# A delta-rule recurrence and a channel mixer on one core: loads reordered at the start, a join's last products rearranged, later due dates for weight slices

## The chip, the core and the metric

The kernel runs on one core of a Trainium2 chip. The metric is the device time of one execution in microseconds. A time given for a kernel is the median over its runs; a profile shows one execution, whose own time is given beside its span. The engines are TensorE (PE, and PEld for its weight loads), VectorE (DVE), ScalarE (ACT), GpSimd (POOL) and SyncE (SP). POOL, SP and ACT also issue the DMA transfers.

## The reference

Two stages follow each other. The first is a delta rule over 768 tokens, for 4 batches of 8 heads with head size 48; the second is a mixer over tokens (low rank) and channels. All numbers are float32.

```python
k_n = k / (norm(k) + 1e-6)
for t in range(S):
    y[:, :, t] = q[:, :, t] @ state
    v_old = state^T @ k_n[:, :, t]
    state += beta[t] * outer(k_n[:, :, t], v[:, :, t] - v_old)
x = y.transpose(0, 2, 1, 3).reshape(4, 768, 384)
u = x + (x^T @ U @ V)^T              # U 768x32, V 32x768
out = u + relu(u @ w_ch1) @ w_ch2    # 384 -> 1536 -> 384
```

The weights, U and V reach the kernel as float64.

## The kernel before, in words

**Units and chunks.** A batch is cut into two units of 384 tokens (`n = 2 b + half`), a unit into six chunks of 64 tokens. Inside a chunk the delta rule is a triangular system: for all eight heads the kernel needs the inverse of a 64x64 unit triangular matrix, kept transposed in `zt`. A unit has 48 such matrices, and they are built like this:

- `load` (L458) brings k, q and v of a unit; `load_beta` (L261) brings beta. For units 0 and 1 q comes as it is and TensorE turns it (`grams`, L519, `turn`, L533); from unit 2 on POOL loads k and q in pieces (`turn_all`, L479, line L495) and VectorE turns them (L504).
- `grams` also makes the products k k^T (`pg`) and k q^T (`qk`), at L562.
- `blocks` (L612) writes `pg` to a scratch in DRAM and reads it back in another layout (`scr<-pg` L634, `gs<-scr` L645), takes the norms (L653 and on), and inverts the diagonal blocks on VectorE in a chain of pairs of operations (L705, L711). For units 0 to 2 the blocks are 16 wide, later 32. The result goes through the scratch again into `zt` (L720, L783).
- `join` (L809) puts blocks together, for units 0 to 2 in three thirds of 16 matrices. Two products with 16-wide blocks (`p_e` L844, `p_d` L856) make 32-wide ones, L860 subtracts, L861 turns the third into `zn` on VectorE, and two products with 32-wide blocks make the off-diagonal block: `p_x` (L867), copied in two halves of 32 partitions on ScalarE (L877), then `p_v` (L883), negated into `zt` in two halves (L889). All of these products are 32x32 tiles of the array. `p_x` and `p_v` have 16 products each, in two of the array's quarters; as float32 products they leave 32 records.

**Recurrence.** `recur(b)` (L906) runs over twelve chunks. Each chunk is a chain across engines: `p_y` from the state (L910), `rhs` on VectorE (L937), `p_s` (L944), `z` on ScalarE (L953), `p_s` (L958) and `p_y` (L966), the new state on VectorE (L981) and the output on ScalarE (L988). A chunk needs its third of the joins.

**Mixer.** `front(b, i)` (L995) makes u for half a batch: `p_tt` (L1008), copied by VectorE (L1014), `p_tt` again (L1017), `p_h` (L1032), added to x (L1038), turned (`p_u`, L1042). `wide(b, i)` (L1053) does the two large products, `p_f` (L1083, with a relu at L1060) and `p_o` (L1104, added at L1065 and stored at L1066).

**Weights.** 14 slices of float64 come in order: four of w1, U, V, two more of w1, six of w2 (`W2` = 8 is the number of the first w2 slice). `start` (L316) issues a load at L337; `one_slice` (L352) turns float64 into float32 with five VectorE operations (L364, L376, L381, L386, L391) and one ScalarE operation (L371). Slices use two buffers, `wide` and `stage` (in two cases an unused part of `w2_sb`), so a load waits until the slice before the last has been converted.

**What sets the order.** A planner written into the kernel. Every part is a generator which yields either a list of events it needs (`need`) or a `step` with its expected cost on each engine. `run` (L158) picks the step that can start first by its own clock; a low place number in `order` (L1116 on) wins when steps compete. `emitted(key, after)` says when an event will be true. So costs and dates in the code issue no work; they decide the order in which instructions stand on each engine. Each engine then works in that order. `fetched` (L146) models that TensorE's instructions come in lots of 256, `ins` being the number in a step. Two gates, `gate` (L413), are small POOL copies that wait for a value of unit 0's inversion (`opened 0`) and for one of the transferred `zt` (`opened 1`); what stands behind them on POOL starts no sooner.

**POOL at the start**, in the order of the program: constants, beta of unit 0, q of unit 0 (8 loads), beta of unit 1, constants and pads (`later_constants`, L244: `quarters`, `mask_e`, `bias_e`, pads of q), weight slice 0, q of unit 1 (8 loads), gate 0, v of unit 0 (8), slice 1, a first four key loads of unit 2 (L495), gate 1, v of unit 1 (8), the remaining twelve.

Of the kernel before, what the change touches and what calls it, by code (L numbers as in the profile page):

```python
# [27 lines left out]
def kernel(  # L28
# [78 lines left out]
    clock = dict(now=0.0, at=0.0, pe=0.0, dve=2.5, act=0.8, sp=0.8, pool=3.8, slow=1.6)  # L107

    LOT, FETCH = 256, 4.1
    lot = dict(since=0.0, used=0)  # L110

# [6 lines left out]
    def step(pe=0, dve=0, act=0, sp=0, pool=0, then=0.0, on=None, take=(), give=(), ins=64):  # L118

        return dict(
            pe=pe, dve=dve, act=act, sp=sp, pool=pool, then=then, on=on, take=take, give=give, ins=ins
        )
# [33 lines left out]
    def run():  # L158

        while waits:  # L160
# [35 lines left out]
            if s["pe"]:  # L196
                fetched(at, s, True)
                ends["pe"] = clock["pe"] = at + s["pe"] * clock["slow"]
            for e in ENGINES[1:]:
                if s[e]:  # L200
                    ends[e] = clock[e] = max(clock[e], ends["pe"]) + s[e]
# [104 lines left out]
    def load_weights():  # L306
# [9 lines left out]
        def start(i):  # L316
            dst, src, groups = slices[i]
            n = dst.shape[1]
            if i in (W2 + 1, W2 + 3):

                at = WIDE * (2 + (i - W2 + 1) // 2)
                wide = early[:, at : at + 2 * n].bitcast(I32)
                wide = wide.rearrange("p (n two) -> p n two", two=2)
            elif i % 2 and i < W2:
                wide = stage[:, 0 : 2 * n].bitcast(I32).rearrange("p (n two) -> p n two", two=2)
            else:
                wide = conv.tile([128, n, 2], I32, name="wide")
            src = src.bitcast(I32)
            to = wide.rearrange("p n two -> p (n two)")
            if groups:  # L330
                to = to.rearrange("p (c r) -> p c r", c=groups)
                src = src.rearrange("(c p) r -> p c r", c=groups)
            copies = 128 // src.shape[0]
            yield step(pool=0.55 * copies)
            for c in range(copies):
                at = slice(c * 128 // copies, (c + 1) * 128 // copies)
                nc.gpsimd.dma_start(out=to[at], in_=src)  # L337
            loaded[i] = wide
            emitted(("sent", i))
            emitted(("landed", i), 6.0)  # L340

        def load_all():
            for i in range(len(slices)):
                last = i - 2 if i < W2 + 5 else i - 1
                yield need(("weights", last), ("q", 0))
                if i > 0:
                    yield need(("opened", int(i > 1)))
                if i == W2 + 1:
                    yield need(*early_used)
                yield from start(i)  # L350
# [107 lines left out]
    def load(n):  # L458
# [12 lines left out]
        if n == 1:  # L471
            yield from load_keys(1)
            yield need(("beta", 1))
# [5 lines left out]
    def turn_all(n):  # L479
# [5 lines left out]
        yield need(("queries turned", n - 1))  # L485
# [33 lines left out]
    def grams(n, place):  # L519
# [24 lines left out]
        def products(c0, i):  # L544
# [4 lines left out]
            yield step(pe=0.6 if n > 2 else 1.1 if n == 2 or i else 0.8, then=0.1, take=banks)  # L549
# [259 lines left out]
    def join(n, third, pg, zt):  # L809

        SB, TQ = BK // 2, CS // 3
# [45 lines left out]
        yield step(dve=1.2, then=-0.75, give=(bank,))  # L859
        nc.vector.tensor_tensor(out=odd, in0=odd, in1=p_d, op=ALU.subtract)  # L860
        turned(zn, zq)  # L861
        yield step(pe=0.65 if n < 2 else 0.55, then=0.4 if n > 1 else 0.1, take=(bank,))
        p_x = ps_of([128, TQ, BK], "p_x")
        for e, (c, j, r) in enumerate(where):
            for g in range(2):
                rows = slice(L * g + BK, L * g + L)
                nc.tensor.matmul(  # L867
                    p_x[L * g : L * g + BK, e],
                    pg[rows, c, j, r, 0:BK],
                    zq[rows, e, BK:L],  # L870
                    start=True,
                    stop=True,
                )
        xz = room([128, TQ, BK], "xz")
        yield step(act=0.75, then=0.1, give=(bank,))
        for g in range(2):
            nc.scalar.copy(xz[L * g : L * g + BK], p_x[L * g : L * g + BK])  # L877
        yield step(pe=0.65 if n < 2 else 0.55, then=0.4 if n > 1 else 0.1, take=(bank,))
        p_v = ps_of([128, TQ, BK], "p_v")
        for e in range(TQ):  # L880
            for g in range(2):
                rows = slice(L * g, L * g + BK)
                nc.tensor.matmul(  # L883
                    p_v[rows, e], zn[rows, e, 0:BK], xz[rows, e], start=True, stop=True
                )
        yield step(act=0.75, give=(bank,))
        for g in range(2):
            rows = slice(L * g, L * g + BK)
            nc.scalar.mul(zq[rows, :, BK:L], p_v[rows], -1.0)  # L889
# [105 lines left out]
    def front(b, i):  # L995
# [7 lines left out]
        if i == 0:  # L1003
# [11 lines left out]
            yield step(pe=0.65, then=0.1, take=("one",), ins=4)  # L1015
# [11 lines left out]
        yield step(pe=0.75, then=0.1, take=("pair", "one"), ins=12)  # L1027
# [8 lines left out]
        def block(e, c):  # L1036
            yield step(dve=0.57, then=0.1, give=((), ("pair",), ("one",))[e])
            nc.vector.tensor_tensor(out=x[:, c], in0=x[:, c], in1=p_hs[e], op=ALU.add)  # L1038
            yield step(pe=0.35, then=0.1, take=("one",), ins=6)
# [76 lines left out]
    order = [(load(0), 2), (later_constants(), 2.04), (recur(0), 2)]  # L1116
    order += [(load_beta(n), (2.02, 2.035)[n] if n < 2 else 2.1 + 0.9 * n) for n in range(2 * B)]
    order += [(grams(0, (2.1, 2.35)), 2.1), (grams(1, (1.97, 2.4)), 1.97)]
    order += [(blocks(0), 2), (blocks(1), 2.52), (load(1), 2.04)]
# [49 lines left out]
```

## Time and profile before

| | |
|---|---|
| median of 8 runs | 655.12 us (650.66 to 660.74) |
| profiled execution: its time / its span | 656.99 us / 655.3 us |
| mean granted TensorE clock | 0.911 of full |
| DMA, mean over the span | 73 GB/s, 47.87 MB |
| p_f (L1083), 576 records | 205.9 us busy |
| p_o (L1104), 576 records | 209.8 us busy |
| first p_s of the recurrence (L944) starts | 49.28 us |
| last rhs of batch 0 (L937) starts | 118.12 us |
| first p_tt (L1008) / first p_f (L1083) starts | 121.37 us / 132.3 us |

The profile's page gives each engine's busy time, then the span in 40 slices of about 16.4 us with a digit per slice for the busy share in tenths. PEclk is the granted clock of TensorE in the same way. The chain of waits follows the work that ended last back from the end; a line has start, length and what it was. A timeline line has start, length, engine, source line, operation, output and input with their shapes, a count, and in brackets how long the engine was idle before and what released it. The table by stages gives, for a stretch of time, each engine's busy time with the number of instructions in brackets (in the order PE, PEld, DVE, ACT, POOL), then the granted clock, the DMA share and GB/s.

### The profile page before, as it was taken

What the parts mean: (1) busy time and instruction counts of PE and PEld (TensorE: products, weight loads), DVE (VectorE), ACT (ScalarE), POOL (GpSimd) and SP (SyncE); (2) the same over time, 40 slices, a digit from 0 to 9 for tenths busy, and PEclk for the clock granted to TensorE, in tenths of its full rate; (3) what the DMA queues carried; (4) which work ended last, traced back from release to release, by engine and by line L of the source; (5) the groups of instructions that cost most, each with busy time, mean ns of one, the idle gap of its engine ahead of it and who ended that gap; (6) DMA issues with size and microseconds to landing.
All of it is one profiled execution on the core that took longest, in us unless ns stands there. A gap on an engine that the chain in (4) does not pass through costs nothing.

```text
span 655.3 us, 20993 instructions
## 1 busy us (share of the span) xinstructions
PE 607.9 (93%) x9312; PEld 381.2 (58%) x9312; DVE 316.8 (48%) x761; ACT 169.2 (26%) x421; POOL 228.4 (35%) x380
## 2 busy tenths in 40 slices
PE   4559878699999999989999999999999999999997
PEld 3458767356655556455655555655565555555554
DVE  3489767885578388427831684388101012000000
ACT  3414444224312321233212321222112211210210
POOL 9654276676452734390557055400000000000000
PEclk9655555789999999979998999999999999999999
DMA  8865455856321812550255026400300000000000
GB/s 129 190 156 126 113 157 112 224 126 121 88 69 38 173 30 56 111 124 3 37 124 122 14 38 119 91 14 2 62 27 14 1 13 13 12 1 24 12 14 24
DMA packets 85163, 47.87 MB, mean 73 GB/s; under 512 B 73584, under 2 KB 78240, under 8 KB 85072
## 3 DMA queue, kind: packets, MB, share of 16 engines
q0 software_dynamic: 14528, 26.98, 17.7%
q1 hardware_dynamic: 65808, 18.86, 13.3%
q8 instruction: 73, 1.20, 0.8%
q10 hardware_dynamic: 4736, 0.69, 0.6%
q14 instruction: 18, 0.15, 0.1%
HBM read 35.49 MB, written 11.01 MB: 71 GB/s over the span
## 4 chain that ended last, share of the span: by engine, by line
PE 84%; DVE 6%; DMA 5%; issue 2%; ACT 1%; SPq 0%; POOL 0%; ACTq 0%; DVEq 0%; POOLq 0%
PE p_f L1083 31%; PE p_o L1104 31%; PE p_y L910 4%; PE p_g L562 3%; PE p_s L944 3%; PE p_s L958 2%; PE p_y L966 2%; PE p_u L1042 1%; PE p_h L1032 1%; PE p_d L856 1%; DVE xt L711 1%; DVE prod L705 1%; DMA wide<-in_moe_w_ch_dram 1%; DMA gs<-scr 1%; PE p_tt L1008 1%
## 5 line engine op out<-in xcount | busy, mean ns | idle before, releaser
L1104 PE MATMUL p_o<-w_sb,h_f 128*128 128x384 f32 x576 | 209.8, 503 | 0.0
L1083 PE MATMUL p_f<-ut,w_sb 128*128 128x384 f32 x576 | 205.9, 504 | 0.0
L1083 PEld LDWEIGHTS p_f<-ut,w_sb 128*128 128x128 f32 x576 | 106.0, 192 | 66.6 <-issue 4.0
L1104 PEld LDWEIGHTS p_o<-w_sb,h_f 128*128 128x128 f32 x576 | 103.3, 191 | 61.4 <-issue 4.0
L1060 ACT ACTIVATE h_f<-p_f 128x384 f32<-128x384 f32 x96 | 47.2, 491 | 181.7 <-PE p_f L1083 181.5
L495 POOL DMA_DIRECT2D qn<-in_k_dram x96 | 58.5, 617 | 56.4 <-DVE prod L705 38.7
L1065 DVE TENSOR_TENSOR x<-x,p_o 128x384 f32<-128x384 f32 x24 | 13.3, 554 | 130.6 <-PE p_o L1104 130.4
L711 DVE TENSOR_TENSOR xt<-xt,prod 96x112 f32<-96x112 f32 (+21 forms) x200 | 63.7, 319 | 6.9
L705 DVE TENSOR_TENSOR prod<-gs,xt 96x112 f32<-96x112 f32 (+21 forms) x200 | 63.0, 315 | 5.1
L434 POOL DMA_DIRECT2D vn<-in_v_dram x64 | 42.3, 671 | 64.2 <-DVE rhs L937 50.8
L495 POOL DMA_DIRECT2D qn<-in_q_dram x96 | 58.8, 623 | 13.0 <-DVE kt L504 9.2
L988 ACT COPY x<-p_y 64x192 f32<-64x192 f32 x96 | 30.1, 313 | 44.3 <-PE p_y L966 42.3
L981 DVE TENSOR_TENSOR s<-s,p_s 128x192 f32<-128x192 f32 x40 | 14.1, 351 | 54.6 <-PE p_s L958 49.8
L937 DVE TENSOR_TENSOR rhs<-vn,p_y 128x192 f32<-128x192 f32 x44 | 15.4, 350 | 47.0 <-PE p_y L910 46.5
L953 ACT COPY z<-p_s 128x192 f32<-128x192 f32 x48 | 15.3, 319 | 78.2 <-PE p_s L944 77.9
L944 PEld LDWEIGHTS p_s<-rhs,zt 64*64 64x64 f32 x704 | 17.1, 152 | 26.2 <-issue 22.8
L434 POOL DMA_DIRECT2D kn<-in_k_dram x48 | 31.4, 664 | 1.1 <-issue 1.0
L944 PE MATMUL p_s<-rhs,zt 64*64 64x48 f32 x704 | 23.0, 248 | 6.9 <-DVE rhs L937 6.3
L958 PEld LDWEIGHTS p_s<-z,kn 64*64 64x64 f32 x704 | 16.5, 153 | 20.7 <-issue 12.0
L910 PEld LDWEIGHTS p_y<-s,kt 48*64 48x64 f32 x704 | 16.7, 152 | 19.3 <-issue 7.5
L966 PE MATMUL p_y<-z,qk 64*64 64x48 f32 x768 | 23.3, 240 | 1.7 <-issue 1.2
L958 PE MATMUL p_s<-z,kn 64*64 64x48 f32 x704 | 22.4, 248 | 2.2 <-ACT z L953 2.2
(126 smaller groups left out, 589.9 us busy)
## 6 DMA issues: line engine op xcount, KB each, us to landing
wide<-in_moe_w_ch_dram POOLq DMA_DIRECT2D x7, 768.0 KB, 6.0
vn<-in_v_dram POOLq DMA_DIRECT2D x64, 72.0 KB, 3.5
out_dram<-x SPq DMA_DIRECT2D x24, 192.0 KB
kn<-in_k_dram POOLq DMA_DIRECT2D x48, 72.0 KB, 3.2
gs<-scr SPq DMA_DIRECT2D x8, 384.0 KB
scr<-xt SPq DMA_DIRECT2D x8, 384.0 KB
scr<-pg SPq DMA_DIRECT2D x30, 96.0 KB
zt<-scr SPq DMA_DIRECT2D x30, 96.0 KB
```

The lines of the kernel that those rows point to most:

```text
L434: engines[queue].dma_start(out=t[half(g ^ (s % 2) if crossed else g), :, s], in_=src[b, 4 * g + s, hf * UC * L : (hf + 1) * UC * L, :].rea ...
L495: nc.gpsimd.dma_start(out=places[rows, x, j, :, 0 : ds.stop - ds.start], in_=src[b, h, hf * UC * L : (hf + 1) * UC * L, ds].rearrange("(m ...
L705: nc.vector.tensor_tensor(out=prod, in0=gb[:, :, j : j + 1, j + 1 :].to_broadcast([NP, split, m, w]), in1=xb[:, :, 0:m, j : j + 1].to_broa ...
L711: nc.vector.tensor_tensor(out=xb[:, :, 0:m, j + 1 :], in0=xb[:, :, 0:m, j + 1 :], in1=prod, op=ALU.subtract,)
L910: nc.tensor.matmul(p[half(x ^ par), par, D * (2 * i + j) : D * (2 * i + j) + D], kq[i][half(par, D), x, j, cu], s_old[half(par, D), x, j], ...
L944: nc.tensor.matmul(p_s[half(x), par, D * (2 + j) : D * (2 + j) + D], zt[half(x ^ par), cu, j, par], rhs[half(x ^ par), 2 * j + par], start ...
L958: nc.tensor.matmul(p_s[half(par), x, D * j : D * j + D], kn[half(x), cu, 2 * j + par], z[half(x), 2 * j + par], start=True, stop=True,)
L966: nc.tensor.matmul(p_y[half(x ^ par), par, D * (2 + j) : D * (2 + j) + D], qk[half(x), cu, par, j], z[half(x), 2 * j + par], start=(c == 0 ...
L988: nc.scalar.copy(tokens_of(b, c, g), pair_of(p_y, 1)[half(g)])
L1060: nc.scalar.activation(hs[f], p_f, ACTF.Relu)
L1083: nc.tensor.matmul(p_f, w1_sb[:, t, f * 128 : (f + 1) * 128], ut[:, t], start=(t == 0), stop=(t == KT - 1),)
L1104: nc.tensor.matmul(p_os[c], hs[e][:, c * 128 : c * 128 + 128], w2_sb[:, e], start=(e == 0), stop=(e == FT - 1),)
```

## The change

- **Loads.** q of unit 1 no longer waits for beta of unit 1, and `load(1)`, `load_beta` and `later_constants` have other places. The first weight slice waits for gate 0, all others for gate 1. `turn_all` of unit 2 waits for gate 1. In the program POOL now issues: beta of unit 0, q of unit 0, q of unit 1, constants and pads, beta of unit 1, gate 0, v of unit 0, slice 0, gate 1, v of unit 1, slice 1, all sixteen key loads of unit 2.
- **Joins of units 0 to 2.** Only the left half of `zn` is turned after the subtraction. `p_x` keeps 16 products: for the first eight matrices into the upper 32 partitions of each half, for the other eight, from `zn`, into the lower ones, so that one copy of 128 partitions with half the elements takes both. `p_v` keeps 16 products too, for the first eight matrices as before and for the others in the other association (`xz` as the weights), alternating between two banks; four negations of half the size follow. In the very first join two of them go to VectorE.
- **Planner.** w2 slices are expected 8.0 instead of 6.0 after their issue; a switch between large and small products costs 0.05 or 0.1 at full clock; a few steps have other costs or other `ins`.

On the engines, the program has as many TensorE instructions as before. On VectorE the first two operations on weight slice 0 stood ahead of unit 0's inversion and now stand in the recurrence with the other three; the first two operations on the second w2 slice stood ahead of the last `rhs` of batch 0 and now stand behind it and behind the turn of unit 2's queries. Around the front of batch 1, where TensorE had p_tt, p_g, p_h, p_u and p_x with no p_o between, seven of the large p_o products now stand among them.

```diff
-    clock = dict(now=0.0, at=0.0, pe=0.0, dve=2.5, act=0.8, sp=0.8, pool=3.8, slow=1.6)
+    clock = dict(now=0.0, at=0.0, pe=0.0, dve=2.5, act=0.8, sp=0.8, pool=3.8, slow=1.6,
+                 big=False)
...
+    SWITCH = 0.05, 0.1
...
+            big=ins < 16,
...
+                if s["big"] != clock["big"] and clock["slow"] == 1.0:
+                    ends["pe"] = clock["pe"] = clock["pe"] + SWITCH[s["big"]]
+                clock["big"] = s["big"]
...
-            emitted(("landed", i), 6.0)
+            emitted(("landed", i), 6.0 if i < W2 else 8.0)
...
-                yield need(("weights", last), ("q", 0))
-                if i > 0:
-                    yield need(("opened", int(i > 1)))
+                yield need(("weights", last), ("opened", int(i > 0)))
...
             yield from load_keys(1)
-            yield need(("beta", 1))
...
-        yield need(("queries turned", n - 1))
+        yield need(("queries turned", n - 1), ("opened", 1))
...
-        yield step(dve=1.2, then=-0.75, give=(bank,))
+        yield step(dve=0.9, then=-0.3, give=(bank,))
         nc.vector.tensor_tensor(out=odd, in0=odd, in1=p_d, op=ALU.subtract)
-        turned(zn, zq)
+        nc.vector.transpose(zn[:, :, 0:BK], zq[:, :, 0:BK])
+        TH = TQ // 2
+        halves = [(slice(L * g, L * g + BK), slice(L * g + BK, L * g + L)) for g in range(2)]
...
-        p_x = ps_of([128, TQ, BK], "p_x")
-        for e, (c, j, r) in enumerate(where):
-            for g in range(2):
-                rows = slice(L * g + BK, L * g + L)
+        p_x = ps_of([128, TH, BK], "p_x")
+        for late in range(2):
+            for e, (c, j, r) in enumerate(where[TH * late : TH * late + TH]):
+                for top, low in halves:
+                    if late:
+                        nc.tensor.matmul(
+                            p_x[low, e], pg[top, c, j, r, BK:L], zn[top, TH + e, 0:BK],
+                            start=True, stop=True,
+                        )
+                    else:
+                        nc.tensor.matmul(
+                            p_x[top, e], pg[low, c, j, r, 0:BK], zq[low, e, BK:L],
+                            start=True, stop=True,
+                        )
+        xz = room([128, TH, BK], "xz")
+        yield step(act=0.35, then=0.1, give=(bank,))
+        nc.scalar.copy(xz, p_x)
...
+        p_vs = [p([128, TH, BK], "p_v") for p in (ps_of, ps_one)]
+        for e in range(TH):
+            for top, low in halves:
                 nc.tensor.matmul(
-                    p_x[L * g : L * g + BK, e],
...
+                    p_vs[0][top, e], zn[top, e, 0:BK], xz[top, e], start=True, stop=True
+                )
                 nc.tensor.matmul(
-                    p_v[rows, e], zn[rows, e, 0:BK], xz[rows, e], start=True, stop=True
-                )
-        yield step(act=0.75, give=(bank,))
-        for g in range(2):
-            rows = slice(L * g, L * g + BK)
-            nc.scalar.mul(zq[rows, :, BK:L], p_v[rows], -1.0)
+                    p_vs[1][top, e], xz[low, e], zq[low, TH + e, BK:L], start=True, stop=True
+                )
+        first = (n, third) == (0, 0)
...
+        for i, p_v in enumerate(p_vs):
+            for top, low in halves:
+                to = zq[top, TH * i : TH * i + TH, BK:L]
+                if first and i:
+                    nc.vector.tensor_scalar_mul(to, p_v[top], -1.0)
+                else:
+                    nc.scalar.mul(to, p_v[top], -1.0)
...
-            yield step(pe=0.65, then=0.1, take=("one",), ins=4)
+            yield step(pe=0.65, then=0.1, take=("one",), ins=16)
...
-        yield step(pe=0.75, then=0.1, take=("pair", "one"), ins=12)
+        yield step(pe=0.75, then=0.1, take=("pair", "one"), ins=16)
...
-            yield step(pe=0.35, then=0.1, take=("one",), ins=6)
+            yield step(pe=0.35, then=0.1, take=("one",), ins=16)
...
-    order = [(load(0), 2), (later_constants(), 2.04), (recur(0), 2)]
-    order += [(load_beta(n), (2.02, 2.035)[n] if n < 2 else 2.1 + 0.9 * n) for n in range(2 * B)]
+    order = [(load(0), 2), (later_constants(), 2.03), (recur(0), 2)]
+    order += [(load_beta(n), (2.015, 2.04)[n] if n < 2 else 2.1 + 0.9 * n) for n in range(2 * B)]
...
-    order += [(blocks(0), 2), (blocks(1), 2.52), (load(1), 2.04)]
+    order += [(blocks(0), 2), (blocks(1), 2.52), (load(1), 2.02)]
```

## The prediction, made before the run

> **What bounds the kernel now.** I read the page first: what share each engine is busy, and how that is spread over the 40 slices.
>
> ```profile
> PE 607.9 (93%) x9312; PEld 381.2 (58%) x9312; DVE 316.8 (48%) x761; ACT 169.2 (26%) x421; POOL 228.4 (35%) x380
> ...
> PE   4559878699999999989999999999999999999997
> ...
> PEclk9655555789999999979998999999999999999999
> ...
> q8 instruction: 73, 1.20, 0.8%
> ```
>
> TensorE is nearly full from slice 9 on (about 132 us), and what it does from there is mostly the mixer's products, which the change leaves alone. Before that, slices 2 to 7, it is partly busy and at half clock. So a gain has to come from the first 132 us, or from holes in the dense stage. The chain of waits up to 50 us shows what sets the start of the recurrence.
>
> ```profile
> 14.34 3.51 DMA scr<-pg
> 17.98 6.09 DMA gs<-scr
> ...
> 25.19 0.20 DVE cp L660
> 25.41 0.25 ACT xt L678
> 25.66 0.81 ACT power L371
> ...
> 26.55 0.20 DVE prod L705
> ...
> 35.13 3.81 DMA scr<-xt
> ...
> 39.32 3.23 DMA zt<-scr
> ```
>
> It is a serial run: two transfers, unit 0's inversion on VectorE (26.55 to 35.1), two transfers, then the first join, which the timeline shows from its last third on.
>
> ```profile
> 45.85 1.06 PE L867 MATMUL p_x<-zt,pg 32*32 32x32 f32 x32 [0.54 <-DVE zt L860]
> 46.96 0.75 ACT L877 COPY xz<-p_x 32x256 f32<-32x256 f32 x2 [2.79 <-PE p_x L867]
> 47.38 1.45 PE L883 MATMUL p_v<-xz,zn 32*32 32x32 f32 x32 [0.46 <-ACT xz L877]
> 48.86 0.77 ACT L889 ACTIVATE zt<-p_v 32x256 f32<-32x256 f32 x2 [1.15 <-PE p_v L883]
> ```
>
> The recurrence starts behind it, at 49.28. Twelve chunks follow, the last one's rhs at 118.12. Its end is spoilt by a transfer: in the timeline VectorE stands in L364 until a w2 slice lands, with rhs queued behind it and TensorE waiting for rhs.
>
> ```profile
> 112.21 0.72 POOL L337 DMA_DIRECT2D w_sb<-in_moe_w_ch_dram  x1
> 117.18 0.56 DVE L364 TENSOR_SCALAR power<-w_sb 128x768 uint16<-128x768 uint16 x1 [3.77 <-DMA w_sb<-in_moe_w_ch_dram]
> 118.12 0.35 DVE L937 TENSOR_TENSOR rhs<-vn,p_y 128x192 f32<-128x192 f32 x1
> 118.61 0.68 PE L944 MATMUL p_s<-rhs,zt 64*64 64x48 f32 x16 [4.05 <-DVE rhs L937]
> ```
>
> The table by stages completes it: 48 to 112 us is at half clock, 270 to 295 us has a hole.
>
> ```profile
> 48.00:112.00 64.00, 53.79 (x1883) 48.03 (x1880) 50.88 (x96) 28.28 (x70) 35.08 (x57) 0.50 0.50 129
> 270.00:295.00 25.00, 22.23 (x417) 12.63 (x418) 7.31 (x13) 8.65 (x21) 21.15 (x33) 0.86 0.67 137
> ```
>
> **The change, part by part** (its own execution: 656.99 us, span 655.3).
>
> **A. Loads at the start.** Unit 1's q is eight issues of 0.66 us on POOL, 72 KB each. They move from 16.1-22.3 to right behind unit 0's q, 10.6-15.9. POOL's 2.8 us of constants and pads (12.8-15.6) and the second beta (2.2 us) slip behind them, to about 18.7 and 21. Who waits: the first transposes of q (17.2) need the pad, so they slip about 1.4 us, with 16 products of k queued behind; their copies sit behind the wait for gs (24.09) on ScalarE anyway, so this is free until gs lands before 20. The second beta is needed at 38.8: free. The first w1 slice (768 KB) leaves the stretch in which gs is read; it goes behind v of unit 0, from 15.6 to about 29. So gs shares the engines with less: it took 6.09 us at 18; the transfer at 416.43, in quiet, let its sqrt start 3.71 us later, the one at 121.72 took 4.25. I take 4.3: -1.8 (bounds -2.4, and +1 if q now slows the scr write before it). The slice's first two operations leave the chain as well: L376 (0.55 us at 25.30) held back L689, on which the inversion waits; prod could start at 26.1: -0.45. Slice 1 and 16 loads of unit 2's keys (9.8 us of POOL) now wait until zt is there, so scr<-xt and zt<-scr are alone with slice 0. The same write at 57.18 and at 458.82 let zt be issued 3.0 us later, against 3.8 here: -0.7. Unit 2's keys then land near 57 and are used at 85.5: free.
>
> **B. The first join.** The p_x copies (two of 0.37) become one over all partitions with half the elements: 0.28 (192 elements take 0.32 at L953, 32 take 0.25 at L678), -0.47. p_v took 1.45 because its second half waited for the second copy; on four quarters I take 0.65, half of p_d's 64 records (1.08, of which 0.24 is the length of a single one): -0.8. The two negations (0.77) are split between ScalarE and VectorE, 0.6: -0.15. p_x keeps its length: each half of it still uses two quarters, and the half that needs the turned zn finds it ready (half a transpose of 0.71, about 0.4, beside the first half). Together -1.4.
> The price of p_v rests on this: p_e puts 64 records on four quarters in about 1.01 us from start to next start, p_x 32 on two quarters in about 1.0, so 16 against 31 ns a record. The Trainium skill (TensorE: Matmul & The Clock Gate, "Wait — 56ns, not 53.3ns?") says that starts never come closer than some 25 ns however small the product. By that rule p_v needs 0.8 us and saves 0.2; by the row of p_e it saves 0.5. The row is the same shape in the same stage: I take it.
> A to B: rhs and all behind it 4.35 us earlier.
>
> **C. Five further joins at half clock.** p_v takes 0.5 less of TensorE each, 2.5 in all. But the instructions stay as many, and TensorE fetches them in 73 blocks over the span (16 KB each, about 255 of its 18,624); its "issue" gaps in 66 to 104 us (1.07, 0.49, 0.85, 1.20, 1.12) stand at such blocks. A faster p_v there only waits longer. I take half: -1.2 (bounds 0 and -2.5). ScalarE: copy 0.28 and four negations of about 0.28 against 1.52: even. VectorE: six half transposes save 1.8, two negations cost 0.5.
>
> **D. Slices and the last chunk.** In the new order the first two operations on the first w2 tile stand behind the last rhs and the turn of q. The wait of 3.77 leaves the recurrence: -3.8. VectorE's load up to that rhs is even: five operations of slice 0 instead of three (+1.1), two of that w2 tile fewer (-1.1). But slice 0 is now converted wholly inside the recurrence, and a load starts only when the last slice but one is out of its buffer; if the recurrence moves up 4 us and the slices by less, the 1.2 us wait at 107.8 grows: +0.5. The last rhs comes 8.9 us earlier, about 109.2. Next late is the w2 tile: issued about 4 us earlier, landing near 113, then four operations (3 us) ahead of the copy of tt, which was at 124.12. That gives back 1.7: tt is 7.2 earlier.
>
> **E. The dense stage.** Three joins at full clock: p_e takes 0.75 for 64 records there, p_v 0.69 for 32, so p_v on four quarters about 0.47: -0.2 each, -0.7 (bounds 0 and -1). The planner's costs of switching, the w2 dates and `ins` issue nothing themselves; they reorder. Around the front of batch 1 the new order puts seven p_o between p_tt, p_h and p_u, where TensorE stood 2.8 us. The clock by five-us stretches (0.92, 0.50, 0.89 from 280 to 295) means 6.9 us at half, 3.4 lost. The skill (same page, "What's actually happening") ties the drop to an idle window of about 3.4 us; the holes here are shorter, each under 1.5 us, and the clock fell all the same. By the rule filling them saves at most 2.8, by the row up to 6.2. I take -2.5, as a second such hole at 345 to 353 (1.3 idle, 1.7 by clock: 3.0) stays to be filled or not; the bound above is +3, another such hole. An order with new delays has waits of its own: +1.5, near the 1.2 row (bounds 0 and +6).
>
> Sum: -7.2 - 0.7 - 2.5 + 1.5 = -8.9. On the profiled execution 648.1; that one lies 1.9 above the median of 655.12, so the median is **646.2**. About 0.5%, 3.3 us, is what a measurement can tell from no change.
>
> **Rivals.**
> 1. *Hidden gain* (0.19): fetches swallow C, q's early loads slow scr as much as gs gains, the hole moves elsewhere. Left are B (-1.4) and part of D (-2): about 652.5. For it: DMA share is 0.9 to 1.2 from 4 to 24 us, so moved bytes only trade places. Against: 768 KB really leave that stretch.
> 2. *Slower, by late slices* (0.11): the two buffers make each load wait for the last conversion but one; slice 2 is issued at 59.4 and its L364 starts at 66.2, one landing (6.0) later, so there is under 1 us to spare. If slice 0's later conversion makes VectorE stand in front of rhs for 2 us at each of slices 2 to 8, that is 7 x 2 = +14: 655.1 - 8.9 + 14 = 660. It decides from about 1.3 us per slice. Against: slice 2's buffer is free at about the same absolute time, as VectorE finishes the inversion earlier. The dense end has room: the last w2 slice is done at 175.0, and the product that needs it comes at about 184.
> 3. *It doesn't do what it says* (part of 1): p_v's two products write the same columns in two banks; if they take turns, B shrinks by 0.5 and C and the -0.7 vanish: 648.6. p_g has that pattern (64 records in 1.09 us at full clock), which speaks against it.
>
> **Chances.** Likeliest case and rival 3: 0.70, faster by over 0.5%; no change 0.19; slower 0.11. From the bounds (A -3.5 to +1, C, E) the likeliest case spans 638.5 to 651.5; stretched over rival 1 the range is 638.5 to 655.
>
> **What would show it.** gs landing within 4.5 us; the first p_s near 45; p_v near 0.65 us; the last rhs near 109 with no L364 wait ahead of it; the first p_f near 125; clock 1.0 through 270-295. Wrong: a first p_s later than 48, L364 waits on slices 1 to 8 summing above 5 us, or a first p_f after 131.

## The result, and the profile after

The changed kernel takes 646.41 us (median of 11 runs, 644.29 to 650.58), the kernel before 653.6 us (median of 32 runs in the same session, 649.79 to 660.74). The ratio is 0.9891, 95% interval 0.986 to 0.9922: 7.1 us less. Disturbed runs are left out of this ratio and of those below. The total is within 0.2 us of the predicted 646.2, but part of that is luck: the prediction started from a median of 655.12 us (8 runs) and took 8.9 off; with 32 runs the median before is 653.6, and 7.1 came off. The parts, too, are not where the prediction put them.

In the page of the changed kernel the second row is TensorE's busy share in 40 slices, the third the granted clock.

```profile
PE 600.8 (93%) x9312; PEld 376.0 (58%) x9312; DVE 315.1 (49%) x763; ACT 167.4 (26%) x428; POOL 229.4 (36%) x380
...
PE   5667687799999999999999999999999999999997
...
PEclk9855555789999999999999999999999999999999
```

From slice 9 to the last but one both rows are nines; before, the busy row had an 8 at slice 17 (counted from 0), the clock row a 7 there and an 8 at slice 21. Slices 2 to 7 look no fuller than before. The table by stages says so in numbers.

```profile
270.00:295.00 25.00, 24.38 (x449) 14.94 (x446) 12.24 (x31) 10.38 (x26) 15.79 (x25) 1.00 0.68 119
46.65:118.88 72.23, 54.70 (x2000) 48.16 (x2001) 55.78 (x105) 30.35 (x83) 41.18 (x66) 0.50 0.56 150
```

The hole at 270 to 295 is closed, with full clock: five p_o products (ten records; the list of the change says seven) now stand between the first p_tt and p_x of that front, as in these lines.

```profile
272.41 0.91 PE L1125 MATMUL p_o<-w_sb,h_f 128*128 128x384 f32 x2
273.25 0.92 PE L1053 MATMUL p_h<-tt,v_sb 32*128 32x384 f32 x6
274.10 0.91 PE L1125 MATMUL p_o<-w_sb,h_f 128*128 128x384 f32 x2
```

The second row of the table is the first recurrence, from the first p_s to the first p_tt: 72.23 us. Before, it ran from 49.28 to 121.37 us, 72.09.

The start, in the chain of waits:

```profile
15.16 4.35 DMA scr<-pg
19.64 3.42 DMA gs<-scr
...
33.81 3.25 DMA scr<-xt
37.44 3.15 DMA zt<-scr
```

gs takes 3.42 instead of 6.09; the scr write ahead of it pays 0.84 of that back and starts 0.8 later. The first join (timeline; p_v has a row per record, of which the first and the last stand here):

```profile
44.11 0.64 PE L883 MATMUL p_x<-zt,pg 32*32 32x32 f32 x16 [0.54 <-DVE zt L866]
...
44.59 0.68 PE L877 MATMUL p_x<-zn,pg 32*32 32x32 f32 x16
...
45.31 0.27 ACT L889 COPY xz<-p_x 128x128 f32<-128x128 f32 x1 [2.87 <-PE p_x L877]
45.62 0.26 PE L894 MATMUL p_v<-xz,zn 32*32 32x32 f32 x1 [0.35 <-ACT xz L889]
...
46.04 0.24 PE L897 MATMUL p_v<-zt,xz 32*32 32x32 f32 x1
...
46.65 0.96 PE L965 MATMUL p_s<-vn,zt 64*64 64x48 f32 x16 [0.37 <-ACT zt L910]
```

p_v runs from 45.62 to 46.28: 0.66 us, where 0.65 was predicted. The first p_s is at 46.65. The end of the recurrence and the first mixer:

```profile
115.52 0.35 DVE L958 TENSOR_TENSOR rhs<-vn,p_y 128x192 f32<-128x192 f32 x1 [1.31 <-PE p_y L931]
...
121.61 0.56 DVE L1035 COPY tt<-p_tt 128x384 f32<-128x384 f32 x1 [0.43 <-PE p_tt L1029]
...
126.80 0.26 ACT L658 ACTIVATE norm<-gs 96x32 f32<-96x32 f32 x1 [7.32 <-DMA gs<-scr]
...
127.61 1.10 PE L1063 MATMUL p_u<-ident,x 128*128 128x128 f32 x6 [1.27 <-ACT ut L1066]
```

The last rhs waits for no slice. But it comes at 115.52, not at 109, and the first p_f follows at 130.85, only 1.4 us earlier than before (132.21). From there to the end before needed 523.1 us and the changed kernel 513.9. The two profiled executions (656.99 and 646.41 us, spans 655.3 and 644.7) are 10.6 us apart, and 9.2 of these lie in the dense stage, for which the prediction had 1.7.

**A ledger of the dense stage.** For every kernel below I took the stretch from the first p_f to the end and split it in three, from the table by stages in steps of 5 us: idle time of TensorE up to its last product, time lost to the clock ((1 - granted clock) x length), and the rest, which is the products at full speed and some 3.7 us after the last one. The clock column has two parts: what was lost in the first 10 us of the stretch, where a half clock from the first mixer's front still runs on, and what was lost later.

| kernel | ratio to before, 95% | first p_s | p_s to p_tt | first p_f | idle | clock | rest |
|---|---|---|---|---|---|---|---|
| before | 1 | 49.28 | 72.1 | 132.2 | 4.4 | 2.7 + 5.1 | 510.9 |
| changed | 0.9891 (0.986-0.9922) | 46.65 | 72.2 | 130.9 | 1.5 | 2.1 + 0 | 510.3 |
| load_only | 0.9984 (0.9959-1.0009) | 47.55 | 71.8 | 129.6 | 5.2 | 0 + 1.7 | 511.1 |
| join_only | 0.9928 (0.9901-0.9954) | 52.22 | 69.9 | 132.9 | 2.2 | 0 + 0 | 509.9 |
| switch_only | 0.9967 (0.9942-0.9992) | 52.40 | 71.9 | 135.0 | 3.4 | 0 + 1.7 | 511.1 |
| w2dates_only | 0.9989 (0.9963-1.0016) | 50.22 | 67.9 | 130.9 | 3.6 | 1.3 + 1.7 | 510.7 |
| load_and_join | 0.992 (0.9887-0.9953) | 46.23 | 73.9 | 130.9 | 2.7 | 2.7 + 3.4 | 509.9 |
| without_w2dates | 0.9919 (0.9885-0.9952) | 45.67 | 73.2 | 129.3 | 2.8 | 0 + 0 | 510.8 |
| without_switch | 1.0001 (0.9965-1.0037) | 46.95 | 72.5 | 131.6 | 6.9 | 2.5 + 5.1 | 510.0 |
| without_join | 0.993 (0.9901-0.996) | 47.89 | 71.2 | 131.4 | 2.2 | 1.5 + 0 | 511.0 |
| old_join_between | 0.9905 (0.9875-0.9934) | 46.93 | 75.1 | 132.6 | 2.0 | 0 + 0 | 510.4 |
| filler_in_hole | 1.0016 (0.9984-1.0049) | 52.26 | 70.4 | 133.4 | 4.3 | 0 + 1.7 | 513.7 |
| pv_three_times | 1.0013 (0.9983-1.0043) | 47.39 | 81.2 | 140.7 | 1.3 | 1.8 + 0 | 510.2 |
| qk_left_out | 0.9873 (0.9835-0.9912) | 47.13 | 68.8 | 128.2 | 2.7 | 2.4 + 0 | 510.5 |

Ratios are from many runs, the other columns from one profiled execution each. A profiled execution can lie off the median of its kernel: those of before, without_switch, switch_only and load_and_join took 2.7 to 4.1 us more, that of without_w2dates 3 less. So a row says where the time of one execution went, and the ratio says what the kernel is worth. The rest lies within 1.2 us in all kernels but filler_in_hole, which has three more products. The parts don't simply add up either: the four single ratios of the next section multiply to 0.987.

### The profile page after: what moved, and what is told of

The parts are those of the page before. It is cut to its first block, busy times and chain, and to the rows that moved or that the text cites. A ratio compares the mean times of both kernels' runs of the same rounds, so it can differ in the third digit from the quotient of the medians.

```text
span 644.7 us, 21001 instructions
## 1 busy us (share of the span) xinstructions
PE 600.8 (93%) x9312; PEld 376.0 (58%) x9312; DVE 315.1 (49%) x763; ACT 167.4 (26%) x428; POOL 229.4 (36%) x380
## 4 chain that ended last, share of the span: by engine, by line
PE 86%; DMA 4%; DVE 4%; issue 2%; ACT 2%; SPq 1%; ACTq 0%; DVEq 0%
PE p_o L1125 31%; PE p_f L1104 31%; PE p_y L931 4%; PE p_g L567 3%; PE p_s L965 3%; PE p_s L979 3%; PE p_y L987 2%; DMA scr<-pg 2%; PE p_u L1063 1%; PE p_d L862 1%; PE p_h L1053 1%; DMA gs<-scr 1%; PE p_e L850 1%; DVE prod L710 1%; DVE xt L716 1%
## 5 line engine op out<-in xcount | busy, mean ns | idle before, releaser
L1104 PE MATMUL p_f<-ut,w_sb 128*128 128x384 f32 x576 | 203.3, 500 | 0.0
L1086 DVE TENSOR_TENSOR x<-x,p_o 128x384 f32<-128x384 f32 x24 | 13.2, 553 | 129.8 <-PE p_o L1125 129.6
L567 PE MATMUL p_g<-qt,kt 48*64 48x64 f32 x768 | 18.8, 246 | 6.3 <-DVE qk L583 5.6
```

What stands on the lines that cost most here:

```text
L567: nc.tensor.matmul(p_g[par][to, c, j], kq[0][rows, x, j, c0 + c], kq[i][rows, x, j, c0 + c], start=True, stop=True,)
L1104: nc.tensor.matmul(p_f, w1_sb[:, t, f * 128 : (f + 1) * 128], ut[:, t], start=(t == 0), stop=(t == KT - 1),)
```

## The experiments

My theory after the result: the gain lies in the dense stage, in gaps of TensorE and the half clock behind them, and the order of p_o there decides it. The rival is the prediction's account: loads, first join and the last chunk's wait. A third question was whether instruction fetch takes back what the joins save.

### One part at a time

load_only: the edit is the new places and needs of the loads.

```diff
-                yield need(("weights", last), ("q", 0))
-                if i > 0:
-                    yield need(("opened", int(i > 1)))
+                yield need(("weights", last), ("opened", int(i > 0)))
...
-            yield need(("beta", 1))
...
-    order += [(blocks(0), 2), (blocks(1), 2.52), (load(1), 2.04)]
+    order += [(blocks(0), 2), (blocks(1), 2.52), (load(1), 2.02)]
```

> The kernel before with only the new order of the loads (q of unit 1 early, v and the slices behind the gates); joins and planner as before. By the prediction's terms: first p_s about 3 us earlier, all of it kept to the end: 650.6 against 653.6. By the rival (the gain of the change lies in the dense stage, where this kernel keeps the order of before, with the hole at the front of batch 1 and half clock behind it): first p_s about 2 us earlier, the stretch from the first p_f to the end stays at 523 us, total -1 to -2.

Measured: 0.9984, not told from 1: what the rival gave. The first p_s is at 47.55. That is 1.7 before the profile of before, but four other kernels have before's loads, and in them it comes at 50.22, 52.26, 52.40 and (with the new join) 52.22. From the start of the scr write to the end of gs the old loads need 9.7, 10.3, 11.8, 11.8 and 12.1 us, the new ones 7.4 to 9.0 in nine kernels. So the loads give about 3 us at the start, as predicted, though the execution that I had predicted from was the luckiest of five. They are not kept to the end: the interval of the ratio allows 2.7 us at most. The dense stage kept the gaps of before (5.2 idle); one profile doesn't show what else took them.

join_only: only the join.

> The kernel before with only the new join. By the prediction's terms: first join -1.4, the five further ones -1.2, the three dense ones -0.7: -3.3, 650.3. By the rival (instruction fetch takes back what the joins save): first p_s -0.7, nothing more by the last rhs, which still waits for the first w2 tile; the hole at the front of batch 1 stays, as no p_o stands between p_tt and p_u in this order: total between -1.5 and 0, and up to -3 more only if the second hole of before (345 to 353 us, 3.0 us with its clock) has happened to close.

Measured: 0.9928, 4.7 us: more than the prediction's terms, and the far end of the rival's, whose condition was met. p_f is not earlier (132.9). The gain is in the dense stage: with other costs in its steps the planner has another order, in which the hole at 345 us is closed, the front of batch 1 has 1.2 us of idle time instead of 2.8 (still without a p_o in it), and no clock is lost. That is neither theory's join, but a new order that came with it.

switch_only: the planner's switch costs and the three `ins`.

```diff
+    SWITCH = 0.05, 0.1
...
+                if s["big"] != clock["big"] and clock["slow"] == 1.0:
+                    ends["pe"] = clock["pe"] = clock["pe"] + SWITCH[s["big"]]
+                clock["big"] = s["big"]
```

> The kernel before with only the planner's costs of a switch between large and small products and the three changed ins; loads, joins and the w2 dates as before. No work is added or removed; p_o products now stand between p_g, p_h and p_u at the front of batch 1. By the prediction's terms: -2.5 for the hole, +1.5 for new waits: -1, 652.6. By the rival: the hole with its half clock is gone, -5 to -6, about 648, clock 1.00 through 270 to 295, everything up to the first p_f as before.

Measured: 0.9967, 2 us, between both. The front of batch 1 is filled, but in this order a gap of 2.25 us opens at 285 us in p_v, ended by nothing that the profile shows ("issue"), and half clock follows it (0.92 and 0.74 in the two stretches from 285 us).

w2dates_only:

```diff
-            emitted(("landed", i), 6.0)
+            emitted(("landed", i), 6.0 if i < W2 else 8.0)
```

> The kernel before with only the w2 slices expected 8.0 instead of 6.0 us after their issue. By the prediction's terms: the wait of 3.77 us ahead of the last rhs goes, 1.7 come back at the copy of tt: -2.1 at the first p_f and at the end, 651.5. By the rival: the same work waits for the same transfers a little later, the first p_f comes 0 to 1.4 earlier; the hole at the front of batch 1 stays open (no p_o between p_tt and p_u in this order either): 0 to -1.4.

Measured: 0.9989. The prediction's step D is right in its place: the recurrence is 4.2 us shorter (72.1 to 67.9; predicted 3.8). But from p_tt to p_f it gives back 1.9 (10.8 to 12.7): p_u waits 2.0 us for a copy of ut that stands on ScalarE behind the norm of unit 2, and that waits for gs. The prediction had 1.7, at another place. In the total it isn't told from nothing.

### Undoing one part

load_and_join undoes the planner's part: switch costs, `ins` and w2 dates.

> The changed kernel with the planner's part undone (no switch costs, w2 dates and ins as before): loads and joins new. If the parts add up as measured singly (0.9984 x 0.9928): ratio 0.991, the last rhs still waiting 3 to 4 us for the w2 tile, the first p_f near 129, the dense stage near 512 us as in the run with the join alone. If the planner's order is what makes the change (its hole filled at the front of batch 1): no better than 0.996.

Measured: 0.992, as the product of the two single ratios. This goes against my theory, which allowed no better than 0.996: without anything of the planner's part the kernel is 1.9 us behind the changed one, and the intervals overlap. Its front of batch 1 has join_only's order and the same gaps (0.64 and 0.57 us). In its profiled execution half clock followed them and cost 3.4 us, in join_only's it did not; that execution took 651.34 us, 4.1 over its kernel's median.

without_w2dates undoes the one line of w2dates_only.

> The changed kernel with only the w2 dates undone. By the prediction's step D: the wait ahead of the last rhs is back (+3.8, -1.7 that the later copy gives back): +2.1 against the changed kernel, ratio about 0.992. If the wait is hidden or comes back elsewhere anyway: the same as the changed kernel, 0.989.

Measured: 0.9919, 1.8 us more than the changed kernel, but the intervals overlap: this decides neither for the 2.1 of step D nor for nothing. In the profile VectorE waits 3.4 us for slices in the recurrence again, which is still only 0.9 us longer (73.2 against 72.2), and p_tt to p_f is 1.5 shorter (10.5 against 12.0). Up to the first p_f the dates give nothing in these two executions.

without_switch undoes the four `SWITCH` edits.

> The changed kernel with only the switch costs of the planner undone; loads, joins, w2 dates and ins as changed. The front of batch 1 has no p_o between p_tt, p_h and p_u again. If the filled front is worth what idle time and half clock of the dense stage show so far (about 7 us in profiles with the open front, about 3.5 with the filled one): +3 to +4 against the changed kernel, ratio 0.994 to 0.995. By the prediction's term (-2.5, and +1.5 for new waits): +1, 0.9905. If the hole is hidden anyway: 0.989.

Measured: 1.0001. The whole gain is gone, 7.2 us (0.011 of 653), twice what I had expected. Everything before p_f is within 0.8 us of the changed kernel (46.95, 72.5, 131.6); the difference is the dense stage. But this holds for these edits together: load_and_join has no switch costs either and keeps the gain. The costs are needed with the new `ins` and w2 dates, not as such. TensorE's timeline has the open front of before again, and further on a gap that the profile puts down to nothing:

```profile
277.53 0.69 PE L560 MATMUL p_g<-kt 48*64 48x64 f32 x32 [1.01 <-DVE kt L501]
...
280.46 0.92 PE L1046 MATMUL p_h<-tt,v_sb 32*128 32x384 f32 x6 [0.30 <-ACT pg L572]
282.03 0.55 PE L1056 MATMUL p_u<-ident,x 128*128 128x128 f32 x3 [0.65 <-DVE x L1052]
283.15 1.34 PE L1056 MATMUL p_u<-ident,x 128*128 128x128 f32 x6 [0.57 <-ACT ut L1059]
```

```profile
345.72 1.16 PE L560 MATMUL p_g<-kt 48*64 48x64 f32 x64
346.81 1.02 PE L745 MATMUL p_x<-zt,pg 32*32 32x32 f32 x96
347.76 0.68 PE L560 MATMUL p_g<-kt 48*64 48x64 f32 x26
350.67 0.34 PE L560 MATMUL p_g<-kt 48*64 48x64 f32 x6 [2.24 <-issue]
```

and half clock behind both, in the table by stages:

```profile
280.00:285.00 5.00, 3.48 (x71) 2.16 (x67) 1.97 (x4) 2.40 (x7) 5.00 (x8) 0.84 0.86 170
285.00:290.00 5.00, 5.00 (x81) 2.81 (x71) 1.48 (x3) 0.48 (x2) 5.00 (x9) 0.50 0.69 150
345.00:350.00 5.00, 3.43 (x189) 2.64 (x188) 0.00 (x0) 1.68 (x5) 5.00 (x9) 1.00 0.60 146
350.00:355.00 5.00, 4.33 (x14) 2.49 (x14) 0.00 (x0) 0.65 (x2) 5.00 (x9) 0.67 0.51 86
```

In the last run of small products 192 records of p_g and p_x stand in a row. With a weight load for each they are 384 instructions in under 3 us, more than one fetch of about 255. The trace also records the transfers of the instruction queue, 73 of 16 KB: one ran from 347.96 to 349.47, and p_g went on at 350.67. In the recurrence of four kernels and the dense stage of five, all 31 "issue" gaps of 0.3 us and more that I compared with these transfers end 1.1 to 1.6 us after one has landed. So I call them fetch gaps. The changed kernel has large products between the same pieces:

```profile
338.48 1.16 PE L567 MATMUL p_g<-kt 48*64 48x64 f32 x64
339.57 2.20 PE L1125 MATMUL p_o<-w_sb,h_f 128*128 128x384 f32 x6
341.71 0.69 PE L567 MATMUL p_g<-kt 48*64 48x64 f32 x32
342.33 2.20 PE L1125 MATMUL p_o<-w_sb,h_f 128*128 128x384 f32 x6
```

six records of p_o take 2.2 us for 12 instructions, and no gap follows.

without_join puts the old join back.

> The changed kernel with the joins as before. By the prediction's terms (first join 1.4, five further ones 1.2, dense ones 0.7): +3.3 against the changed kernel, ratio 0.994. If instruction fetch takes all that the five further joins save: p_s +1.4, the recurrence not longer than in the changed kernel (72.2 us from the first p_s to the first p_tt), the dense stage +0.7: +2, 0.992. If the join alone (0.9928 measured singly) keeps its size beside the rest: +4.7, 0.996.

Measured: 0.993, 2.5 us from the changed kernel, nearest to the second of the three expectations (0.992), though the intervals exclude none of them. In the profile p_s is 1.24 later, the recurrence 1.05 shorter (71.2), p_f 0.6 later, the rest of the dense stage 0.7 longer, as the second has it.

old_join_between has the new join only in the first join and in the dense stage (`if n >= 2 or (n, third) == (0, 0)`).

> The changed kernel with the join of before in the five joins that stand inside the first recurrence, the new one in the very first join and in the dense stage. If fetch takes back what those five save and nothing else is lost by them: the same as the changed kernel, 0.989, with 3 us more busy time and 3 us less of issue gaps from the first p_s to the first p_tt. If the new join's four copies on ScalarE ahead of z lengthen the chunks (72.2 us in the changed kernel against 67.9 with the w2 dates alone): 2 to 4 us less than the changed kernel, 0.983 to 0.986. By the prediction's step C: 1.2 more, 0.991.

Measured: 0.9905, not told from the changed kernel, nor from the 0.991 of step C; only the third expectation is out. Its recurrence is 75.1 us, with 58.4 busy and 8.4 of issue gaps, so the exchange that I expected (less gaps for more busy time) isn't there, and neither is a shorter recurrence. This kernel's order in the recurrence differs in other ways too (slices' operations stand elsewhere around the last rhs).

### Measuring a cost by itself

filler_in_hole puts three products that nobody reads into the gaps of before at the front of batch 1.

```diff
+    def fill(spare, times):
+        for _ in range(times):
+            nc.tensor.matmul(
+                spare[:, 0, 0:DM], w1_sb[:, 0, 0:128], w2_sb[:, 0], start=True, stop=True
+            )
```

> The kernel before with three products whose result nobody reads (128x384, 0.85 us each) in the gaps at the front of batch 1: after the first p_tt, after p_h and after the first p_u. It does 2.5 us more work and closes 2.2 us of idle. If the hole costs more than its idle time because TensorE falls to half clock behind it: granted clock 1.00 from 270 to 295 us in spite of the added work, time 1.5 to 5 us less than before. If it costs its idle time alone: 0 to +1 us.

Measured: 1.0016. This is what idle time alone gives, but the experiment doesn't tell what it should: the filler stands in the chain p_tt, p_g, p_h, p_u and moved the gaps instead of closing them. p_g waits 0.77 for the copy of pg, p_h 0.77 again, the clock drops to 0.75 and 0.91, and the fetch gap further on (2.07) stays.

pv_three_times and qk_left_out ask what binds the recurrence.

```diff
-        for e in range(TH):
+        for again in range(3 if n < 2 else 1):
+            for e in range(TH):
```

> The changed kernel with the p_v products of the six joins of units 0 and 1 issued three times (same operands, same result): 64 records more per join, 128 instructions, 768 in all. If the early stage is bound by what the array takes for the records (16 ns each): about 1 us per join, +6 in all. If it is bound by the fetch of instructions (three more lots of 255, one lot per 4.1 to 4.7 us): +12 to +14, with more issue gaps on TensorE between 46 and 120 us.

```diff
-            for j, par, x in heads:
+            for j, par, x in heads if b > 0 or c == 0 else ():
                 nc.tensor.matmul(
                     p_y[half(x ^ par), par, D * (2 + j) : D * (2 + j) + D],
                     qk[half(x), cu, par, j],
```

> The changed kernel with the products of z and qk left out in chunks 1 to 11 of batch 0: its output lacks that summand there. They stand behind p_s in each chunk, where TensorE next waits for VectorE's new state, so that they are not on the chain of a chunk; but they are 352 instructions, 1.4 lots. If the recurrence is bound by the fetch of instructions: 5 to 6 us less than the changed kernel, 0.980 to 0.982. If it is bound by the chain of waits from engine to engine: 0 to 1 us less.

The recurrence in the two, in the table by stages (span, then busy time and records of TensorE):

```profile
47.39:128.56 81.17, 59.65 (x2320) 52.30 (x2320) 55.83 (x105) 30.10 (x83) 40.02 (x64) 0.52 0.51 137
```

```profile
47.13:115.97 68.84, 50.09 (x1824) 43.72 (x1825) 55.99 (x106) 30.32 (x83) 40.65 (x66) 0.50 0.60 158
```

With 640 instructions more (five joins; the first lies ahead of p_s) it is 8.9 us longer: 4.95 busy, and 5.1 more of issue gaps (8.3 to 13.4). With 352 less it is 3.4 shorter, though I had taken those products to be off the chain of a chunk. Both lie between the two expectations: the recurrence pays 10 to 14 ns for an instruction more or less, against 18 for the mean one (72.2 us for 4,001). Of the 8.9 us more 5.1 are fetch gaps; of the 3.4 less it is 1.1 (8.3 to 7.2). Fetch is a part of what binds the recurrence, not all. In the total the first kernel is 8.0 us behind the changed one by the ratios, the second 1.2 ahead, which isn't told from nothing.

The waits of TensorE in the recurrence show it, before (first) and changed:

```profile
PE p_s L944 <- DVE rhs L937: 6.3, 5, 4.1
PE p_s L958 <- ACT z L953: 2.2, 4, 0.6
PE p_y L966 <- issue: 1.2, 1, 1.2
PE p_d L856 <- issue: 1.1, 1, 1.1
PE p_x L867 <- issue: 1.1, 1, 1.1
```

```profile
PE p_s L965 <- DVE rhs L958: 3.9, 7, 0.7
PE p_s L979 <- ACT z L974: 3.0, 5, 0.9
PE p_y L931 <- issue: 3.0, 2, 2.8
PE p_d L862 <- issue: 2.2, 1, 2.2
PE p_s L965 <- issue: 1.6, 1, 1.6
```

The wait of 4.1 for the last rhs is gone, and the issue gaps have grown from 4.7 in all to 8.3.

## Why the prediction was right in its total and wrong in its parts

- **A, loads.** Right in kind. Against before's profile p_e came 2.0 earlier where 2.95 was predicted: gs saved more than said (2.7 against 1.8), the scr write paid 0.84 back (it stood in the bounds), and it began 0.8 later, which I hadn't reckoned with. From gs to the inversion 0.3 was saved (0.45 predicted), in the two transfers behind it 0.6 (0.7). Against the five kernels with old loads the step is worth about 3. (The DMA share that rival 1 gives as 0.9 to 1.2 from 4 to 24 us is 0.63 from 12 to 16.)
- **B, first join.** 0.9 instead of 1.4. From the start of p_x to p_s it took 3.43 in before and in four more kernels with the old join (3.84 in load_only, with a fetch gap in p_x); with the new one 2.50 to 2.74. p_v had its price: 32 records on four quarters in 0.66, starts 13.5 ns apart on average (45.62 to 46.04), where the Trainium skill (TensorE: Matmul & The Clock Gate, "Wait — 56ns, not 53.3ns?") has about 25 at the least; this case's rows decide against that figure. What failed is the -0.47 for the xz copy. It was counted twice: before, p_v began behind the first half of that copy, and its 1.45 us contained the wait for the second. From p_x to the start of p_v it took 1.53 before and 1.51 after.
- **C, five further joins.** Predicted -1.2; from before to changed the recurrence gained nothing. Busy time in it fell by 3.1, a little more than the 2.5 of the working; issue gaps rose by 3.6. Four pairs of kernels differ in the join alone: busy time fell by 2.7 to 3.7 in all of them, issue gaps rose by 1.6, 3.0 and 2.7 in three, and the recurrence changed by -2.2 (join_only), +2.1 (load_and_join), +1.0 (against without_join) and -2.9 (against old_join_between). So the shorter products are real, and what is left of them is smaller than the effect of the other order that comes with them: -0.5 on average, told neither from 0, as rival 1 had it, nor from -1.2.
- **D, last chunk.** The wait (for the second w2 slice) went, -4.2 where it was the only edit. But in the changed kernel undoing it lengthens the recurrence by 0.9 only: TensorE waits 1.8 us more for rhs, with 0.8 less of busy time and 0.4 less of issue gaps. And 1.5 to 1.9 come back between p_tt and p_f. In the changed kernel half of the 1.5 is the wait for ut (1.27 against 0.57); the other half is the p_h behind it, 1.95 us for what takes 1.10 in without_w2dates, as at half clock. Net about 0 instead of -1.6. This and C are most of why p_f came at 130.9 and not at 125.
- **E, dense stage.** The -0.7 for the three joins is right: the rest column is 511.0 on average in five kernels with the old join (before, load_only, switch_only, w2dates_only, without_join) and 510.2 in the eight with the new one. The failed term is the hole: "-2.5" with "+1.5" for new waits. In the two profiles idle fell by 2.9 and clock loss by 5.7, of which 5.1 stood behind the two holes. I had seen 6.2 for the first hole and 3.0 for the second in the rows, took 2.5 of 9.2, and granted 1.5 to new waits, of which one of 0.57 (at 416 us) came. Of the two readings that I had set side by side for the first hole, 2.8 by idle time alone and 6.2 with the clock, the second was the nearer: in the changed kernel 0.6 of idle time is left at that front, and no clock is lost. Part of the 9.2 is luck of that one execution: load_only had the same front and lost nothing to the clock there.

So the early part gave 1.4 (two profiles) to 2.3 us (first p_f at 131.2 in changed and without_switch, at 133.5 in the three with before's loads, join and dates) instead of 7.2, and the dense stage the remaining 5 or so of the median instead of 1.7. The two errors, 5 us too much and 3 too little, cancelled for the most part, and the 1.8 left over was nearly made up by the 1.5 by which before's median had moved. Of the signs named, gs, p_v, the missing wait and the clock at 270 to 295 came true; the first p_s (45), the last rhs (109) and p_f (125) did not. The limit of a first p_f at 131, past which I would have called the prediction wrong, was kept by 0.15 us.

**What is shown and what stays open.** Shown: the time of these kernels goes with the idle time of the dense stage. In the order of that column the kernels that do the full work once, 1.5 to 2.2 us idle, have ratios of 0.989 to 0.993; 2.7 and 2.8 have 0.992; 3.4 and 3.6 have 0.997 and 0.999; 4.4 to 6.9 have 0.998 to 1.000. From 1.5 to 4.4 us idle the time rises by 7 us, some 2 of them from the early part, and from there to 6.9 no further. Shown too: taking the switch costs out of the changed kernel takes the gain away.

Shown as a pattern of all traces, though no experiment moved a single gap: half clock in the dense stage follows idle time, by the rule in the last section. With 3.4 us idle or more all six kernels lost clock there, with 2.8 or less one of eight. So which order the planner lands on is worth more than the steps of the prediction, and the same order of one front can cost 3.4 us in one execution and nothing in another.

Not shown: that the order is better because the switch is priced rightly. Alone the price gave a third of what its absence costs, since it opened a gap of its own, and load_and_join does without it. Open too: what becomes of the 3 us that the loads save at the start, and what the five further joins are worth.

## What to carry to other kernels

A planner's costs are also a choice of order: even an edit far away (the join) reshuffled a stage 200 us later by more than its own saving, so judge it by the gaps of that stage, not by the work that it removes. Where a stage has fetch gaps, count instructions beside array time: cheaper products may only wait longer at the next block. And take the price of a step from several executions, since single profiles were 3 us apart at the start and 6 in the clock.

## What the hardware showed that I had not expected

- In the new join the first eight p_x products needn't hold up the other eight. Where zn was ready, their records interleave in the timeline though the program has one set after the other: both together take 0.9 us (79.24 to 80.13), between the 1.06 of before's 32 records on two quarters and the 0.66 of p_v's 32 on four.
- The granted clock of a profile can be wrong where its record is missing. switch_only's record begins at 129 us, and its rows say 1.00 for the whole start; but p_tt takes 2.77 us there, as at half clock (2.66 in the changed kernel, where the row says 0.50), against 1.48 later on. I take its early part as half clock.

```profile
112.00:130.00 18.00, 12.81 (x320) 9.19 (x313) 13.34 (x22) 6.68 (x16) 11.01 (x17) 1.00 0.69 169
```

```profile
124.34 2.77 PE L1015 MATMUL p_tt<-x,u_sb 128*32 128x384 f32 x12
```

- Which gap drops the clock can be read from the traces. Each has a record of when the clock changed, and in each trace all changes lie on one grid of 3.41 us. I laid that grid over TensorE's busy time, as the profile counts it, from 100 us to its last product: some 2,100 stretches at full clock in fourteen traces. Of the 20 that were less than 0.63 busy, 18 were followed by half clock; of those 0.64 busy or more, not one. The two exceptions are without_join at 284.5 us (0.54) and filler_in_hole at 345.8 (0.55). In the dense stage a fall lasts one or two stretches and so costs 1.7 or 3.4 us. Here are the stretches of before's first hole, of without_switch's fetch gap and of a like gap of 2.00 us in without_w2dates:

```profile
277.42:280.83 3.41, 3.11 (x99) 1.88 (x91) 0.56 (x1) 1.85 (x6) 3.41 (x6) 1.00 0.55 137
280.83:284.24 3.41, 1.95 (x57) 1.34 (x57) 1.97 (x4) 1.34 (x3) 3.41 (x6) 1.00 0.98 189
284.24:287.66 3.42, 3.42 (x80) 1.98 (x69) 0.86 (x2) 0.48 (x1) 3.42 (x6) 0.50 0.68 114
...
348.27:351.68 3.41, 1.17 (x15) 0.71 (x9) 0.00 (x0) 0.70 (x3) 3.41 (x6) 1.00 0.27 61
351.68:355.09 3.41, 3.41 (x7) 1.89 (x6) 0.00 (x0) 0.02 (x1) 3.41 (x7) 0.50 0.70 115
...
334.59:338.00 3.41, 2.59 (x187) 2.34 (x186) 0.00 (x0) 1.68 (x5) 3.41 (x6) 1.00 0.54 144
338.00:341.42 3.42, 2.24 (x11) 1.45 (x12) 0.00 (x0) 0.65 (x2) 3.42 (x6) 1.00 0.27 62
```

The second gap lies within one stretch (1.17 of 3.41 busy), and the clock falls. The third is split between two (0.76 and 0.65 busy), and the next stretch has full clock. The same order of join_only and load_and_join left 0.65 in the one and 0.61 in the other, which alone fell. So what a gap costs depends on where it meets the grid.
